# Softplus written back into its PSUM bank, in a kernel of attention, a mixture of experts and a second MLP

## The chip, the core and the metric

The kernel runs on one core of a Trainium2 chip. The metric is the device time of one execution in microseconds, the median of several runs. A page of the profile and a trace come from one more execution, recorded by the hardware profiler.

## The reference

Three stages follow each other. `x` goes from one to the next as 2304 rows of 512 numbers; everything is float32.

```python
# attention over keys and values averaged in groups of 8
attn = softmax(q @ pooled_k.T / 8);  x = attn @ pooled_v      # 4 batches, 8 heads, 576 x 64
# mixture of 8 experts; P comes from 8 rounds of row and column normalisation of exp(x @ w_gate)
for e in range(8):
    h = np.maximum(x @ w1[e], 0.0);  out += P[:, e:e+1] * (h @ w2[e])
# second MLP, with softplus
h = x @ w_in                                                  # 512 -> 2048
g = np.maximum(h, 0.0) + np.log1p(np.exp(-np.abs(h)))
out = g @ w_out                                               # 2048 -> 512
```

The change touches the line with `g`, in the second MLP alone.

## The kernel before

**Engines.** TensorE (PE) multiplies, ScalarE (ACT) applies functions and casts, VectorE (DVE) and GpSimd (POOL) do arithmetic on tiles, SyncE (SP) issues most transfers. PE writes its products to PSUM, which has eight banks of 128 partitions by 512 float32; all other tiles lie in SBUF. GpSimd works on SBUF tiles alone here.

**Precision.** Each float32 operand of a product is split in two: a rounded part (`hi`, type float32r) and a remainder (`lo`). A product is then three matmuls, hi·hi, lo·hi and hi·lo (`three`, L527). So each block of hidden values needs, after its function, a cast (the `hi` part, tile `hhi`) and a subtraction (the `lo` part, tile `hlo`).

**Phases and units.** The tokens are cut in three groups of 768. The work after attention is six phases: the experts for groups 0, 1 and 2 ("moe", 32 units each), then the second MLP for groups 1, 2 and 0 ("sp", 8 units each). A unit takes 256 hidden columns. `first(n)` makes the four hidden blocks of 128 x 384 of unit n with seven products of 6 matmuls (Strassen's scheme; the sums `pa`, `pb`, `pc`, `pd` lie in four banks of kind "p"), so 42 matmuls of 384 columns. `second(n, i)`, for i from 0 to 5, multiplies 128 tokens by the unit's 256 rows of the second weight: 6 matmuls of 512 columns into a bank `py`, which is then added to an accumulator `g` in SBUF (L630 in moe; L615 in sp, but a copy on ScalarE, L613, in the first unit of an sp phase).

**Order.** The kernel writes its order out by hand: `first(n+1)`, then `second(n, 0)` to `second(n, 5)`, then `first(n+2)`, and so on. After `first(n+1)` the activation of its block (0, 0) is issued; the other three are taken from the list `pending`, one behind each of `second(n, 0)`, `second(n, 1)`, `second(n, 2)`. Each engine works its own list in that order. There are three banks of kind "y": `py` of i takes the bank that `py` of i-3 gave back, and gives it back when the addition into `g` has read it. So on VectorE's list a remainder `hlo` stands between two of these additions.

**Weights of the next unit.** ScalarE casts them (`w1hi`, L194; `w2hi`, L202) and GpSimd subtracts (`w1lo`, `w2lo`, helper L165), while `second` runs.

**Side work.** `hook()` takes one entry of a list `side` at each call. In an sp phase it is called 14 times in `first` and 6 times in `second`, in a moe phase 7 and 6 times. At the start of the first two sp phases the list holds the preparation of the next token group: 6 transposes with copies (`pt`, L636, L637), 8 sums (`xs`, L464, L467) and 14 remainders (`xh` on ScalarE, L498; `xl` on VectorE, L503), with empty entries between. That is 92 entries. Their banks `pt`, `xs` and `xh` come from the same three "y" banks as `py`.

**The activation.** `relu` reads its bank twice: ScalarE writes `hhi` from it (L542), and VectorE makes `hlo` from the bank and `hhi` (L543). `softplus` has an extra tile `g` of 128 x 384 float32 in SBUF (tag `sp`, two buffers): ScalarE writes it from the bank (L550), ScalarE casts it to `hhi` (L551), and VectorE subtracts `hhi` from it (L552).

Of the kernel before, what the change touches and what calls it, by code (L numbers as in the profile page):

```python
# [9 lines left out]
F32 = mybir.dt.float32  # L10
F32R = mybir.dt.float32r
U32 = mybir.dt.uint32
AF = mybir.ActivationFunctionType
ALU = mybir.AluOpType
# [5 lines left out]
def attention_moe_softplus_kernel(  # L20
# [12 lines left out]
    nc = tc.nc  # L33
# [512 lines left out]

    def softplus(at, src):
        hh, hl = at
        g = tpool.tile(list(src.shape), F32, tag="sp", name="sp")
        nc.scalar.activation(g, src, AF.Softplus)  # L550
        nc.scalar.copy(hh, g)  # L551
        nc.vector.tensor_tensor(hl, g, hh.bitcast(F32), op=ALU.subtract)  # L552

    def first(n, between):

# [249 lines left out]
    tpool = None  # L805
# [35 lines left out]
    for step, (what, n) in enumerate(todo):  # L841
# [35 lines left out]
        else:  # L877
# [19 lines left out]
            if f + 1 < len(phases) and u == (20 if f == 0 else 8 if kind == "moe" else 0):  # L897
# [5 lines left out]
                else:  # L903
                    g = acc_at[phases.index(("moe", npair))]
# [7 lines left out]
            if attn_m[0] is None and "" in banks:  # L912
                part_banks()
                tpool = pools[0]
# [32 lines left out]
```

## Time and profile before

| | |
|---|---|
| median of 3 runs | 2119.74 us (2118.05 to 2121.77) |
| the profiled execution | 2116.47 us |
| its span, first to last instruction | 2114.7 us |
| TensorE busy | 2024.2 us, 96% |
| VectorE, ScalarE, GpSimd busy | 1442.5, 829.6, 1278.0 us |
| mean granted TensorE clock | 0.985 |

The attention stage fills about the first 105 us (parts of it run on beside the first expert phase), the expert phases last until about 1650 us, and the second MLP fills the rest. Busy times are sums over all of these, so a change in the last stage is read from that stage's rows. In the rows below, a number in square brackets behind an instruction is the time that its engine stood idle before it, and what ended that. [...]

### The profile page before, as it was taken

The page shows a single profiled execution, that of the slowest core. Times are in us where ns is not written, and L with a number is a line of the kernel's source. Part 1 is how long each engine was busy: PE and PEld are TensorE (multiplying, and loading weights), DVE is VectorE, ACT ScalarE, POOL GpSimd, SP SyncE. Part 2 cuts the span into 40 slices and gives each one's busy share as a digit, 9 for nine tenths or more (in the row PEclk, how much of TensorE's full clock was granted, in tenths as well). Part 3 has the DMA queues.
Part 4 walks back from the last instruction along what each step waited for, and adds up shares of the span by engine and source line. Part 5 has one row for each costly group of instructions (what it writes and reads, how often), then busy time and mean ns, then how long its engine had stood idle before and what let it go on. Part 6 is the DMA issues. An engine that isn't in the chain of part 4 may idle for free.

```text
span 2114.7 us, 28374 instructions
## 1 busy us (share of the span) xinstructions
PE 2024.2 (96%) x10643; PEld 1789.4 (85%) x10643; DVE 1442.5 (68%) x2417; ACT 829.6 (39%) x1607; POOL 1278.0 (60%) x1069
## 2 busy tenths in 40 slices
PE   8799999999999999999999999999999988988998
PEld 6687899889889898888898988989889867867877
DVE  3777567776665776677777676667775576576666
ACT  3554434323434224333233333342233554554532
POOL 6654555666665766666666666567576554554653
PEclk8899999999999999999999999999999998999999
DMA  6342221233333333323324333223232323323321
GB/s 175 81 114 70 81 65 60 80 95 110 107 105 109 101 99 113 109 96 99 108 93 152 100 100 92 87 95 109 90 100 85 102 73 105 117 70 126 99 60 60
DMA packets 142311, 205.70 MB, mean 97 GB/s; under 512 B 27916, under 2 KB 88796, under 8 KB 142172
## 3 DMA queue, kind: packets, MB, share of 16 engines
q1 hardware_dynamic: 132092, 190.12, 29.0%
q10 hardware_dynamic: 10080, 13.77, 1.8%
q8 instruction: 83, 1.36, 0.3%
q14 instruction: 56, 0.46, 0.1%
HBM read 173.76 MB, written 30.09 MB: 96 GB/s over the span
## 4 chain that ended last, share of the span: by engine, by line
PE 76%; DVE 10%; POOL 5%; ACT 5%; issue 3%; DMA 1%; ACTq 0%; SPq 0%; POOLq 0%; DVEq 0%
PE py L527 36%; PE p L527 36%; DVE hlo L552 4%; POOL w1lo L165 2%; ACT w1hi L194 2%; DVE g L615 1%; PE s L314 1%; ACT hhi L551 1%; PE px L352 1%; POOL w2lo L165 1%; DVE p L570 1%; POOL sums L165 1%; ACT sp L550 1%; DMA f<-in_moe_w_out_dram 1%; PE pa L342 1%
## 5 line engine op out<-in xcount | busy, mean ns | idle before, releaser
L527 PE MATMUL py<-w2hi,hhi 128*128 128x512 f32 x1440 | 573.6, 398 | 55.1 <-DVE g L615 46.7
L165 POOL TENSOR_TENSOR w1lo<-w1raw,w1hi 128x512 fp32r<-128x512 f32 x240 | 242.5, 1031 | 594.3 <-ACT w1hi L194 594.3
L527 PE MATMUL p<-xhi,w1hi 128*128 128x384 f32 x1680 | 568.4, 338 | 10.6 <-DVE p L570 5.2
L527 PE MATMUL py<-w2hi,hlo 128*128 128x512 f32 x1440 | 569.5, 395 | 0.0
L527 PE MATMUL p<-xlo,w1hi 128*128 128x384 f32 x1680 | 565.4, 337 | 3.8 <-DVE xlo L479 3.8
L527 PE MATMUL py<-w2lo,hhi 128*128 128x512 f32 x1440 | 568.9, 395 | 0.0
L527 PE MATMUL p<-xhi,w1lo 128*128 128x384 f32 x1680 | 565.4, 337 | 3.0 <-POOL w1lo L165 3.0
L630 DVE SCALAR_TENSOR_TENSOR g<-py,prob,g 128x512 f32<-128x512 f32 x468 | 350.0, 748 | 94.0 <-PE py L527 83.0
L527 PEld LDWEIGHTS py<-w2hi,hhi 128*128 128x128 f32 x1440 | 273.1, 190 | 130.9 <-DVE g L615 64.1
L527 PEld LDWEIGHTS p<-xhi,w1hi 128*128 128x128 f32 x1680 | 316.9, 189 | 28.8 <-DVE p L570 7.8
L542 ACT ACTIVATE hhi<-p 128x384 fp32r<-128x384 f32 x384 | 180.8, 494 | 391.0 <-PE p L527 347.4
L527 PEld LDWEIGHTS p<-xlo,w1hi 128*128 128x128 f32 x1680 | 317.0, 189 | 14.4 <-DVE xlo L479 4.5
L527 PEld LDWEIGHTS py<-w2hi,hlo 128*128 128x128 f32 x1440 | 273.0, 190 | 58.8
L527 PEld LDWEIGHTS p<-xhi,w1lo 128*128 128x128 f32 x1680 | 317.1, 189 | 3.6 <-POOL w1lo L165 3.6
L527 PEld LDWEIGHTS py<-w2lo,hhi 128*128 128x128 f32 x1440 | 273.3, 190 | 48.7
L165 POOL TENSOR_TENSOR w2lo<-w2raw,w2hi 128x1024 fp32r<-128x1024 f32 x120 | 294.5, 2455 | 17.1 <-ACT w2hi L202 17.1
L165 POOL TENSOR_TENSOR w1lo<-sums,w1hi 128x1024 fp32r<-128x1024 f32 x120 | 289.0, 2409 | 0.0
L572 ACT COPY za<-p 128x384 f32<-128x384 f32 x120 | 57.8, 482 | 573.7 <-PE p L527 573.7
L543 DVE SCALAR_TENSOR_TENSOR hlo<-p,hhi 128x384 fp32r<-128x384 f32 x384 | 211.0, 550 | 28.9 <-ACT hhi L542 28.8
L570 DVE TENSOR_TENSOR za<-p,za 128x384 f32<-128x384 f32 x120 | 66.9, 557 | 215.1 <-PE p L527 215.1
L552 DVE TENSOR_TENSOR hlo<-sp,hhi 128x384 fp32r<-128x384 f32 x96 | 132.3, 1380 | 39.1 <-ACT hhi L551 39.1
L570 DVE TENSOR_TENSOR u<-p,za 128x384 f32<-128x384 f32 x120 | 66.8, 557 | 123.9 <-PE p L527 94.5
(111 smaller groups left out, 2093.9 us busy)
## 6 DMA issues: line engine op xcount, KB each, us to landing
w1raw<-in_moe_w_dram SPq DMA_DIRECT2D x96, 512.0 KB
w2raw<-in_moe_w_dram SPq DMA_DIRECT2D x96, 512.0 KB
xlod<-xl ACTq DMA_DIRECT2D x70, 192.0 KB
xlo<-xlod SPq DMA_DIRECT2D x35, 384.0 KB
w1raw<-v SPq DMA_DIRECT2D x24, 512.0 KB
w2raw<-v SPq DMA_DIRECT2D x24, 512.0 KB
f<-in_moe_w_in_dram SPq DMA_DIRECT2D x16, 512.0 KB
v<-dt SPq DMA_DIRECT2D x32, 256.0 KB
```

What stands on the lines that cost most here:

```text
L165: nc.gpsimd.tensor_tensor(o, a, b, op=ALU.subtract)
L194: nc.scalar.copy(at(hi), src)
L314: nc.tensor.matmul(ps[:QP, j * 2 * SP:(j + 1) * 2 * SP], qT[:, j * QP:(j + 1) * QP], kb)
L342: nc.tensor.transpose(pa[:SP, j * QP:(j + 1) * QP], ex[:, 2 * j + h, :], ident[:QP, :QP])
L352: nc.tensor.matmul(px[h * D:(h + 1) * D, :W], vp[:, h, :], aT[:, h, :])
L527: nc.tensor.matmul(ps, lhs[a], rhs[b], start=first and i == 0, stop=last and i == 2, skip_group_check=goes_on,)
L542: nc.scalar.activation(hh, src, AF.Relu)
L543: nc.vector.scalar_tensor_tensor(hl, src, 0.0, hh.bitcast(F32), op0=ALU.max, op1=ALU.subtract)
L552: nc.vector.tensor_tensor(hl, g, hh.bitcast(F32), op=ALU.subtract)
L570: add = lambda o, x, y: nc.vector.tensor_tensor(o, x, y, op=ALU.add)
L572: nc.scalar.copy(a, pa)
L630: nc.vector.scalar_tensor_tensor(a, py, prob[:, t, e:e + 1], a, op0=ALU.mult, op1=ALU.add)
```

## The change

The tile `g` goes. ScalarE writes the softplus back into the bank that it read, casts from there, and VectorE subtracts with the bank as its first operand.

```diff
     def softplus(at, src):
         hh, hl = at
-        g = tpool.tile(list(src.shape), F32, tag="sp", name="sp")
-        nc.scalar.activation(g, src, AF.Softplus)
-        nc.scalar.copy(hh, g)
-        nc.vector.tensor_tensor(hl, g, hh.bitcast(F32), op=ALU.subtract)
+        nc.scalar.activation(src, src, AF.Softplus)
+        nc.scalar.copy(hh, src)
+        nc.vector.tensor_tensor(hl, src, hh.bitcast(F32), op=ALU.subtract)
```

No instruction is added, taken away or moved on any engine: 96 softplus, 96 casts and 96 subtractions stand where they stood, with other operands. ScalarE's list in the middle of the last sp phase, from a unit's second block on to the next unit's first (`p_...` are the four banks of a unit), before:

```order
L550 ACTIVATE sp<-p_19048 128x384
L551 CAST hhi<-sp 128x384
L550 ACTIVATE sp<-p_19050 128x384
L551 CAST hhi<-sp 128x384
L202 CAST w2hi<-w2raw 128x1024
L550 ACTIVATE sp<-p_19049 128x384
L551 CAST hhi<-sp 128x384
L572 COPY za<-p_19188 128x384
```

and after:

```order
L549 ACTIVATE p_18964<-p_18964 128x384
L550 CAST hhi<-p_18964 128x384
L549 ACTIVATE p_18966<-p_18966 128x384
L550 CAST hhi<-p_18966 128x384
L202 CAST w2hi<-w2raw 128x1024
L549 ACTIVATE p_18965<-p_18965 128x384
L550 CAST hhi<-p_18965 128x384
L571 COPY za<-p_19100 128x384
```

Only the operands differ (the line numbers fall by one, and the banks' numbers count fewer tiles). A bank of kind "p" is now read last by VectorE's subtraction, where ScalarE's softplus read it last, so it is that which TensorE must wait for before it writes the bank again. The waits of TensorE's matmuls into the second and third bank of a unit in the same phase, before:

```order
L527 MATMUL p_18012<-xhi,w1hi 128x384 [waits Activation_49]
L527 MATMUL p_18012<-xlo,w1hi 128x384
L527 MATMUL p_18012<-xhi,w1lo 128x384 [waits Pool_49]
L527 MATMUL p_18013<-xhi,w1hi 128x384 [waits Activation_49]
L527 MATMUL p_18013<-xlo,w1hi 128x384
```

and after:

```order
L527 MATMUL p_17956<-xhi,w1hi 128x384 [waits Activation_49]
L527 MATMUL p_17956<-xlo,w1hi 128x384
L527 MATMUL p_17956<-xhi,w1lo 128x384 [waits Pool_49]
L527 MATMUL p_17957<-xhi,w1hi 128x384
L527 MATMUL p_17957<-xlo,w1hi 128x384
```

(rows between the two banks' first matmuls repeat and are left out). The matmul into the third bank has lost its wait for ScalarE and got none for VectorE, since a matmul ahead of it in the list waits for a later VectorE instruction already. The wait that stays at the second bank is for the weights' cast.

## Rows read from the trace of the kernel before

**Rows 1.** The page: busy tenths of TensorE in 40 slices of the span.
```profile
PE   8799999999999999999999999999999988988998
```
**Rows 2.** Windows, one of sp, one of moe: length, busy of each engine, clock.
```profile
1656.50:2110.40 453.90, 403.34 (x1920) 347.08 (x1918) 295.03 (x389) 211.76 (x396) 238.75 (x181) 0.97 0.27 86
...
1000.00:1640.00 640.00, 637.45 (x3202) 574.63 (x3202) 454.41 (x778) 221.01 (x409) 418.64 (x347) 1.00 0.32 102
```
**Rows 3.** Waits of PE, 1650 to the end: total us, times, longest.
```profile
PE py L527 <- DVE g L615: 46.7, 35, 3.7
```
**Rows 4.** Timeline of a plain sp unit: start, length, instruction, [idle before].
```profile
2043.54 2.40 POOL L165 TENSOR_TENSOR w1lo<-sums,w1hi 128x1024 fp32r<-128x1024 f32 x1
...
2043.72 2.63 DVE L552 TENSOR_TENSOR hlo<-sp,hhi 128x384 fp32r<-128x384 f32 x1 [0.78 <-ACT hhi L551]
2044.11 0.51 ACT L551 CAST hhi<-sp 128x384 fp32r<-128x384 f32 x1
2044.53 1.05 ACT L202 CAST w2hi<-w2raw 128x1024 fp32r<-128x1024 f32 x1
2045.90 2.69 POOL L165 TENSOR_TENSOR w2lo<-w2raw,w2hi 128x1024 fp32r<-128x1024 f32 x1
2046.28 0.68 DVE L615 TENSOR_TENSOR g<-py,g 128x512 f32<-128x512 f32 x1
...
2046.88 2.13 DVE L552 TENSOR_TENSOR hlo<-sp,hhi 128x384 fp32r<-128x384 f32 x1
...
2047.01 0.50 PE L527 MATMUL py<-w2hi,hhi 128*128 128x512 f32 x1 [0.55 <-DVE g L615]
...
2049.67 0.50 PE L527 MATMUL py<-w2hi,hhi 128*128 128x512 f32 x1 [0.99 <-DVE g L615]
```
**Rows 5.** Tiles: count, min/median/max ns, first and last start, forms.
```profile
L527 PE MATMUL py<-w2hi,hlo x1440: 387/389/632, 111.9 to 2110.0; 128*128 128x512 f32 x180
L543 DVE SCALAR_TENSOR_TENSOR hlo<-p,hhi x384: 512/549/560, 100.6 to 1647.2; 128x384 fp32r<-128x384 f32 x192
L552 DVE TENSOR_TENSOR hlo<-sp,hhi x96: 541/832/2634, 1657.6 to 2099.5; 128x384 fp32r<-128x384 f32 x96
...
L503 DVE TENSOR_TENSOR xl<-g,xh x70: 536/545/555, 532.5 to 1934.3; 128x384 fp32r<-128x384 f32 x70
...
L550 ACT ACTIVATE sp<-p x96: 476/488/493, 1656.5 to 2097.9; 128x384 f32<-128x384 f32 x96
L551 ACT CAST hhi<-sp x96: 511/513/515, 1657.0 to 2098.5; 128x384 fp32r<-128x384 f32 x96
...
L542 ACT ACTIVATE hhi<-p x384: 470/492/532, 96.4 to 1646.1; 128x384 fp32r<-128x384 f32 x192
...
L464 ACT COPY xs<-g x40: 474/487/508, 500.7 to 1869.3; 128x384 f32<-128x384 f32 x40
```
**Rows 6.** Timeline of ACT: the copy `za`, once in each unit.
```profile
1385.77 0.48 ACT L572 COPY za<-p 128x384 f32<-128x384 f32 x1 [2.29 <-PE p L527]
1401.90 0.48 ACT L572 COPY za<-p 128x384 f32<-128x384 f32 x1 [3.44 <-PE p L527]
...
1635.76 0.48 ACT L572 COPY za<-p 128x384 f32<-128x384 f32 x1 [5.93 <-PE p L527]
1651.30 0.48 ACT L572 COPY za<-p 128x384 f32<-128x384 f32 x1 [4.70 <-PE p L527]
...
2087.81 0.48 ACT L572 COPY za<-p 128x384 f32<-128x384 f32 x1 [5.01 <-PE p L527]
```
**Rows 7.** Chain of waits: four transposes in moe, and the last matmuls.
```profile
1304.35 0.44 PE pt L636 x4
...
2095.40 15.02 PE py L527 x66
```
**Rows 8.** Timeline of an sp unit with side work.
```profile
1737.61 2.57 DVE L552 TENSOR_TENSOR hlo<-sp,hhi 128x384 fp32r<-128x384 f32 x1 [1.08 <-ACT hhi L551]
...
1740.83 0.79 PE L527 MATMUL py<-w2hi,hhi 128*128 128x512 f32 x1 [3.69 <-DVE g L615]
```

## The prediction, made before the changed kernel ran

> **What bounds the kernel now.** I read the page's slices first [rows 1]: TensorE is busy for nine tenths or more in every slice from the third to the 32nd, and falls to eight in most of those after that. The sp phases lie there, and `softplus` runs nowhere else. Then a window of each kind [rows 2]: of 640 us of moe TensorE is idle for 640 - 637.45 = 2.6 us, at a clock of 1.00; of 453.9 us of sp for 453.9 - 403.34 = 50.6 us, at 0.97. So TensorE bounds moe, and something else bounds sp.
>
> TensorE's waits name it [rows 3]: 46.7 of the 50.6 us are 35 waits for L615, the addition that gives a `py` bank back. What makes L615 late is read from one unit [rows 4]. Its subtraction `hlo` starts at 2043.72, while GpSimd works on a `w1lo` from 2043.54 to 2045.94, and ends at 2046.35, 0.4 us after it. The next starts at 2046.88 under a `w2lo` that ends at 2048.59, and ends at 2049.01, again 0.4 us after it. The additions queue behind both, and TensorE waits 0.55 and 0.99 us for them. By tile, L552 takes 0.54 us at least, 0.83 in the median and 2.63 at most, while L543 and L503, which read one operand from a bank, stay within 0.51 and 0.56 us in 384 and 70 instructions [rows 5], though GpSimd is at work for 418.61 of 640 us there [rows 2]. So the subtraction with two operands in SBUF is what GpSimd holds up; one with an operand in PSUM is not.
>
> **How much time there is to win.** `za` starts once in each unit. In moe the period is 1651.30 - 1635.76 = 15.54 us [rows 6]. From 1651.30 to 2087.81 there are 23 sp periods: 436.51 us. At TensorE's pace they would take 23 x 15.54 = 357.4 us, and the 48 transposes of the side work 12 x 0.44 = 5.3 us [rows 7], together 362.7. The excess is 73.8 us. It splits in 50.6 us of waits, 453.9 x 0.03 = 13.6 us of lower clock [rows 2], and a rest of 9.6 us: 0.25 us behind each of some 39 waits, where the first matmul takes 0.50 us [rows 4] rather than the usual 0.39 [rows 5]. The lower clock belongs to the long waits: after 3.69 us without work the first matmul takes 0.79 us [rows 8]. Behind 2087.81 there is nothing to win: the last 66 matmuls run without a gap in 15.02 us, 0.228 each [rows 7].
>
> **The change, part by part.**
>
> *The subtraction.* 96 times it gets one operand from a bank. Nearest rows: L503, the same operation with one operand in each memory, 0.536 to 0.555 us, and L543, 0.512 to 0.560. I take 0.55. Bounds: 0.51, and 0.83 with 2.63 at most, as now, if the hold-up has another cause (rival B). In a plain unit [rows 4]: subtraction from 2043.72 to 2044.27, addition (0.68) to 2044.95; the next cast ended at 2044.62, so subtraction to 2045.50 and addition to 2046.18. TensorE wanted the first bank at 2047.01 - 0.55 = 2046.46 and will want the second 6 x 0.228 = 1.37 us later, at 2047.83. Both are free 1.5 us early, so a plain unit waits for nothing and runs at 15.54 us.
>
> [...]
>
> *The softplus and the cast.* ScalarE in place in a bank is not in the trace. It reads a bank and writes SBUF in 0.488 us (L550) and reads SBUF and writes a bank in 0.487 (L464). If reading and writing go on together, 0.47 to 0.51 us; if they take turns, the sum, 0.98. I take 0.49, since each of the two rows already reads and writes at once. The cast from a bank should take 0.47 to 0.53 (L542) rather than 0.513 (L551): nothing. What hides ScalarE now is its idle time (211.76 us busy of 453.9 [rows 2]). At 0.98 the second block's subtraction comes 0.5 and the third's 1.0 us later, within the 1.5 us that the plain unit has left; in units with side work it would add about 0.7 us each.
>
> *The tile `g`.* With it goes ScalarE's wait for one of its two buffers. The bank is held longer instead, until the subtraction. The fourth block is the last: its subtraction would end at about 2047.2 in the unit of [rows 4] (its softplus follows the weight cast that ends at 2045.58, and softplus, cast and subtraction are 1.55 us), and TensorE's next product into that bank starts 12 matmuls after the next unit's first, which follows six matmuls from 2047.83, so not before 2049.2. The 12 take (15.54 - 36 x 0.228) / 42 = 0.175 us each, which makes it 2051.3. Four microseconds are left, and TensorE's list holds no new wait there.
>
> *GpSimd* gets its time back too (a `w2lo` takes 2.69 us here), but nothing waits for it in sp. *Transfers* must bring a unit's weights each 15.54 us instead of each 436.51 / 23 = 19.0: moe does the same at that pace.
>
> **What stays.** In the two batches of side work `xh`, `xs` or `pt` takes one of the three "y" banks between two `py`, so that TensorE waits for an addition one step earlier. 92 entries at 20 a unit are 4.6 units a batch, 9.2 in all (these counts are from the code). Three prices. From moe, where the side work makes a period 16.13 us (1401.90 - 1385.77 [rows 6]): 0.6 x 9.2 = 5.4 us. From the sp unit of [rows 8]: the subtraction there shrinks by 2.57 - 0.55 = 2.0 us, which leaves 3.69 - 2.0 = 1.7 of the wait, so 1.7 x 9.2 = 15.6. Between them: moe's 0.6 at 20 calls a unit instead of 13, 0.6 x 20 / 13 = 0.9, and some 0.2 for the cast that stands in ScalarE's chain beside the softplus, so 1.1 x 9.2 = 10 us. I take 10. Waits of that size cost no clock: after 0.99 us the first matmul takes 0.50 us [rows 4], after 3.69 us 0.79 [rows 8].
>
> **Sum.** 2116.47 (profiled execution; 1.8 us of it outside the span) - 73.8 + 10 = 2052.7 us. The median shown is 2119.74, 3.3 us above that execution, and the changed kernel is timed like the median: 2056, rounded to 2055. From the two ends for the side work, 2119.74 - 73.8 + 5.4 = 2051 to 2061; with nothing left over 2046, with ScalarE at 0.98 us in place 2061 + 6 = 2067. The forecast's own range is 2046 to 2067.
>
> **Rivals.**
>
> *A, the stall moves into the side work.* The longer ScalarE chain (softplus, then cast) and the shared "y" banks become the wait in the 9.2 units: 3 us each, and some lower clock again, about 30 to 35 us stay. For it: these units wait longest now (3.69 us against 0.99). Against: moe, with the same banks, loses 0.6 us a unit. 2119.74 - 73.8 + 33 = 2079, or 2067 to 2080.
>
> *B, the subtraction stays held up* because it is the read of `hhi` or the write of `hlo` in SBUF that GpSimd delays, not the pair of operands. Then nothing goes: 2116 to 2121. Against it stand 454 instructions of L543 and L503 that read and write SBUF in the same way and never take over 0.56 us.
>
> *C, slower: the banks come back too late.* TensorE waits at the head of a unit until VectorE has subtracted the last block. It costs time only if that subtraction is over 4 us later than worked out above, and to lose the 73.8 us again a further 73.8 / 23 = 3.2 us a unit. So from 7.2 us of delay on the kernel is slower; at 8 us it is about 2119.74 + 23 x 0.8 = 2138. For it: VectorE's list is in order, and all else waits on it. Against: without the hold-up VectorE has far less to do than TensorE (295.03 of 453.9 us even with it [rows 2]). [...]
>
> **How the numbers follow.** The forecast gets 0.84, A 0.10, B 0.03, C 0.03. A measurement of this kernel tells about 0.2% (4.2 us) from no change. Forecast and A are faster: 0.94; B is the same: 0.03; C slower: 0.03. The range reaches from 2044, a little below the time with nothing left over, to 2074, which takes in the forecast's upper end and half of A.
>
> **What the profile of the changed kernel would show.** Right: L551 (now the subtraction) 96 times within 0.51 and 0.57 us; TensorE's waits for L614 (now the addition) down from 46.7 to about 10 us, all in the units with side work; `za` periods of 15.54 us in plain units; a clock near 1.00 in sp. ScalarE's softplus at about 0.49 us shows the in-place price right, 0.98 wrong. The prediction is wrong if the subtraction still takes over 1 us under GpSimd's work (B), if 3 us waits stay in the side work (A), or if matmuls into the "p" banks wait for VectorE's subtraction (C).

## The result, and the profile after

| | before | changed |
|---|---|---|
| median | 2120.55 us (4 runs, 2118.05 to 2121.77) | 2062.34 us (4 runs, 2060.18 to 2067.60) |
| ratio | | 0.9731, 95% interval 0.9709 to 0.9752 |
| profiled execution, its span | 2116.47, 2114.7 us | 2063.60, 2061.8 us |

The kernel is 58 us faster. That is about 7 us short of the 2055 us that were forecast, and within the range of 2044 to 2074. (The median of before has one run more than in the table ahead of the prediction.)

TensorE's row of the page's 40 slices has lost its dip in the sp phases [rows 1]:

```profile
PE   8898999999999999999999999999999999999999
```

The next row is a window up to the last matmul (length, busy of each engine with its count, then clock, DMA share, GB/s). It starts 6.2 us ahead of the first softplus, where the window of before starts with it; TensorE works through these 6.2 us without a gap. So the two can be compared in what TensorE does not do: 401.00 - 389.85 = 11.2 us without work, where it was 50.6, at a clock of 1.00 for 0.97 [rows 2] (the granted share of TensorE's clock, a mean over the window). VectorE is busy for 219.61 us in place of 295.03:

```profile
1656.50:2057.50 401.00, 389.85 (x1956) 347.85 (x1954) 219.61 (x392) 207.09 (x398) 220.95 (x184) 1.00 0.31 99
```

What TensorE waited for in that stretch, in all, times, longest [rows 3]:

```profile
PE py L527 <- DVE g L614: 8.9, 8, 1.6
PE py L527 <- DVE g L467: 2.3, 2, 1.1
```

The tile view of the activation (count, then min/median/max ns) answers to [rows 5]. The subtraction has a spread of 17 ns, where it had one of 2.1 us:

```profile
L549 ACT ACTIVATE p<-p x96: 458/482/502, 1662.7 to 2043.8; 128x384 f32<-128x384 f32 x96
L550 ACT CAST hhi<-p x96: 478/480/483, 1663.2 to 2044.3; 128x384 fp32r<-128x384 f32 x96
L551 DVE TENSOR_TENSOR hlo<-p,hhi x96: 543/556/560, 1663.7 to 2046.0; 128x384 fp32r<-128x384 f32 x96
```

The timeline of a plain unit answers to [rows 4]. GpSimd is at work on the same tiles at the same place, and all three subtractions under it take 0.55 to 0.56 us; no matmul into `py` waits in this unit:

```profile
2012.60 2.42 POOL L165 TENSOR_TENSOR w1lo<-sums,w1hi 128x1024 fp32r<-128x1024 f32 x1
...
2012.76 0.56 DVE L551 TENSOR_TENSOR hlo<-p,hhi 128x384 fp32r<-128x384 f32 x1 [0.69 <-ACT hhi L550]
...
2013.24 0.68 DVE L614 TENSOR_TENSOR g<-py,g 128x512 f32<-128x512 f32 x1
...
2013.84 0.55 DVE L551 TENSOR_TENSOR hlo<-p,hhi 128x384 fp32r<-128x384 f32 x1
...
2014.98 2.40 POOL L165 TENSOR_TENSOR w2lo<-w2raw,w2hi 128x1024 fp32r<-128x1024 f32 x1
...
2015.50 0.56 DVE L551 TENSOR_TENSOR hlo<-p,hhi 128x384 fp32r<-128x384 f32 x1 [0.52 <-ACT hhi L550]
```

The copy `za`, once a unit, answers to [rows 6]. The first row is the first sp unit, the next three lie in the first batch of side work, the last two at the end:

```profile
1657.48 0.48 ACT L571 COPY za<-p 128x384 f32<-128x384 f32 x1 [4.70 <-PE p L527]
...
1725.73 0.48 ACT L571 COPY za<-p 128x384 f32<-128x384 f32 x1 [4.98 <-PE p L527]
1743.18 0.48 ACT L571 COPY za<-p 128x384 f32<-128x384 f32 x1 [3.64 <-PE p L527]
1760.63 0.48 ACT L571 COPY za<-p 128x384 f32<-128x384 f32 x1 [3.64 <-PE p L527]
...
2019.41 0.48 ACT L571 COPY za<-p 128x384 f32<-128x384 f32 x1 [3.95 <-PE p L527]
2034.95 0.48 ACT L571 COPY za<-p 128x384 f32<-128x384 f32 x1 [3.95 <-PE p L527]
```

From the first to the last of the 24 it is 377.47 us, for 436.51 before: 59.0 us less. Against the 362.7 us of TensorE's own pace an excess of 14.8 us is left of 73.8. Plain units have the period 15.54. Of each batch of side work, the unit with the transposes has 20.2 (some 2.65 us of it are the transposes themselves, half of the prediction's 5.3), the next 16.95, and two with remainders to make have 17.45. In one of these two TensorE waits once, where it waited 3.69 us [rows 8]:

```profile
1737.67 0.50 PE L527 MATMUL py<-w2hi,hhi 128*128 128x512 f32 x1 [1.57 <-DVE g L614]
```

The two profiled executions differ by 52.9 us and not by 59.0, since the first sp unit starts 6.2 us later in the new one (1657.48 for 1651.30).

### The profile page after: what moved, and what is told of

It reads as the page before. It is cut to its first block, busy times and chain, and to the rows that moved or that the text cites. A ratio compares the mean times of both kernels' runs of the same rounds, so it can differ in the third digit from the quotient of the medians.

```text
span 2061.8 us, 28361 instructions
## 1 busy us (share of the span) xinstructions
PE 2010.8 (98%) x10643; PEld 1788.7 (87%) x10643; DVE 1364.5 (66%) x2417; ACT 822.5 (40%) x1607; POOL 1258.2 (61%) x1069
## 4 chain that ended last, share of the span: by engine, by line
PE 83%; DVE 5%; POOL 5%; ACT 3%; issue 3%; DMA 1%; SPq 0%; ACTq 0%; DVEq 0%; POOLq 0%
PE py L527 41%; PE p L527 37%; POOL w1lo L165 2%; PE s L314 1%; ACT w1hi L194 1%; PE px L352 1%; POOL w2lo L165 1%; PE pk L297 1%; POOL sums L165 1%; PE pa L342 1%; DMA f<-in_moe_w_out_dram 1%; DVE p L569 1%; DVE za L569 0%; PE pq L283 0%; DMA f<-in_moe_w_in_dram 0%
## 5 line engine op out<-in xcount | busy, mean ns | idle before, releaser
L527 PE MATMUL py<-w2hi,hhi 128*128 128x512 f32 x1440 | 565.9, 393 | 15.7 <-DVE g L614 8.9
L165 POOL TENSOR_TENSOR w1lo<-w1raw,w1hi 128x512 fp32r<-128x512 f32 x240 | 241.8, 1029 | 556.1 <-ACT w1hi L194 556.1
L165 POOL TENSOR_TENSOR w2lo<-w2raw,w2hi 128x1024 fp32r<-128x1024 f32 x120 | 289.5, 2412 | 14.8 <-ACT w2hi L202 14.8
L165 POOL TENSOR_TENSOR w1lo<-sums,w1hi 128x1024 fp32r<-128x1024 f32 x120 | 289.4, 2411 | 0.0
L202 ACT CAST w2hi<-w2raw 128x1024 fp32r<-128x1024 f32 x120 | 126.5, 1054 | 0.0
```

The lines of the kernel that those rows point to most:

```text
L165: nc.gpsimd.tensor_tensor(o, a, b, op=ALU.subtract)
L202: nc.scalar.copy(hi, raw)
L527: nc.tensor.matmul(ps, lhs[a], rhs[b], start=first and i == 0, stop=last and i == 2, skip_group_check=goes_on,)
```

## The experiments

Two questions were open: is it GpSimd's reading that held up a subtraction with two operands in SBUF, and what makes the 14.8 us that stay? All medians are of several runs, with the kernel before run beside them on the same chip (2120.8 to 2121.9 us). "Excess" is the time from the first to the last `za` of the sp phases over 362.7 us, in the profiled execution.

| run | median us | ratio to before, 95% interval | excess us | first `za` at |
|---|---|---|---|---|
| before | 2120.55 | 1 | 73.8 | 1651.30 |
| changed | 2062.34 | 0.9709 to 0.9752 | 14.8 | 1657.48 |
| e0_again | 2060.35 | 0.9704 to 0.9733 | 14.8 | 1654.31 |
| e1_four_buffers | 2119.45 | 0.9984 to 1.0004 | 73.2 | 1656.29 |
| e2_write_only | 2064.22 | 0.9721 to 0.9750 | 17.4 | 1655.43 |
| e8_fill_beside | 2065.31 | 0.9716 to 0.9754 | 16.3 | 1658.17 |
| e3_copy_to_bank | 2081.31 | 0.9800 to 0.9830 | 33.0 | 1657.02 |
| e7_no_softplus | 2052.79 | 0.9660 to 0.9686 | 6.6 | 1656.43 |
| e4_side_bank | 2052.00 | 0.9655 to 0.9682 | 6.2 | 1657.16 |
| e5_late_w1 | 2062.88 | 0.9709 to 0.9735 | 15.1 | 1656.47 |
| e6_both | 2051.11 | 0.9651 to 0.9677 | 3.1 | 1656.73 |

**e0_again: the changed kernel once more.**

> The changed kernel once more, word for word. It asks where the part of the time lies that the sp phases don't explain: in the first trace of the changed kernel its first sp unit starts 6.2 us later than in that of before (za at 1657.48 against 1651.30), though nothing ahead of it was changed. Theory: the opening attention stage differs from execution to execution, so the start of the first sp unit moves by some us again, while the stretch from the first to the last za stays at 377.5 us within 1 us. Rival: the change itself costs those 6 us, and the first sp unit starts at 1657 to 1658 again, and at 1651 in every kernel that keeps the tile g. Time 2060 to 2068.

The first and the last `za` of its sp phases:

```profile
1654.31 0.48 ACT L571 COPY za<-p 128x384 f32<-128x384 f32 x1 [4.70 <-PE p L527]
...
2031.78 0.48 ACT L571 COPY za<-p 128x384 f32<-128x384 f32 x1 [3.95 <-PE p L527]
```

The stretch is 377.47 us again, to the hundredth, while its start moved by 3.2 us. The table's last column has 1654.3 to 1658.2 in all new executions, in the three that subtract from `g` in SBUF as before too (e1, e2, e8). So the opening varies whatever `softplus` does, and the profiled execution of before was an early one. The difference is there before the expert phases are under way: their first subtraction `hlo` starts at 100.6 us in the execution of before, at 107.0 in that of the changed kernel and at 104.3 in this one.

**e1_four_buffers: before, with four buffers for `g`.**

```diff
-        g = tpool.tile(list(src.shape), F32, tag="sp", name="sp")
+        g = tpool.tile(list(src.shape), F32, tag="sp", name="sp", bufs=4)
```

> The kernel before, with four buffers for the tile g in place of two, so that ScalarE's softplus never waits for VectorE's subtraction; the subtraction still has both operands in SBUF. Theory (GpSimd holds up a subtraction with two operands in SBUF): the subtraction still takes up to 2.6 us, TensorE still waits about 45 us for the additions, 2112 to 2121 us. Rival (the change won by taking away the wait for one of two buffers): 2060 to 2080 us.

Its subtraction, from the tile view, and TensorE's waits in sp:

```profile
L552 DVE TENSOR_TENSOR hlo<-sp,hhi x96: 540/832/2634, 1662.6 to 2103.9; 128x384 fp32r<-128x384 f32 x96
```
```profile
PE py L527 <- DVE g L615: 45.9, 34, 3.7
```

Both are those of before, and so is the time. The tile's two buffers were no part of the stall.

**e2_write_only: before, with GpSimd filling `w1lo` and `w2lo` with zeros in the sp phases.**

```diff
-            pool_sub(at(lo), src, at(hi).bitcast(F32))
+            if sets[n][1] == "sp":
+                nc.gpsimd.memset(at(lo).bitcast(F32), 0.0)
+            else:
+                pool_sub(at(lo), src, at(hi).bitcast(F32))
```

(and likewise for `w2lo`)

> The kernel before, in which GpSimd fills w1lo and w2lo of the sp phases with zeros where it made them by a subtraction; so the remainders of those weights are left out of the result. GpSimd still writes the same tiles in SBUF but reads nothing for them. Theory (it is GpSimd's reading that holds up VectorE's second operand in SBUF): the subtraction hlo stays near 0.54 us except under the four short sums of a unit, which still read, and the time falls to 2055 to 2070 us. Rival (any work of GpSimd in SBUF, writes too, holds it up): the subtraction is stretched by the length of a fill, and with fills of about 1 us the time is 2080 to 2115 us.

The time is what the theory said, but the run doesn't tell the two apart. A fill waits for no cast, so it ran at another time than the subtractions, as the timeline of a unit shows (its last subtraction, then the fills):

```profile
2016.26 0.56 DVE L558 TENSOR_TENSOR hlo<-sp,hhi 128x384 fp32r<-128x384 f32 x1 [0.59 <-ACT hhi L557]
...
2018.18 1.67 POOL L196 MEMSET w1lo<- 128x512 f32 x3
2019.79 0.96 POOL L207 MEMSET w2lo<- 128x1024 f32 x1
```

What it shows is that with GpSimd's long subtractions gone the old `softplus`, with `g` in SBUF, is nearly as fast as the new one: 2 us more in the median, 2.6 in the excess. The tile view has a spread left:

```profile
L558 DVE TENSOR_TENSOR hlo<-sp,hhi x96: 541/558/1125, 1661.7 to 2046.6; 128x384 fp32r<-128x384 f32 x96
```

The subtractions over 0.56 us, up to 1.12, are all among the 22 that started under one of GpSimd's short sums (L162, L165), which still read; the 66 with no work of GpSimd beside them take 0.55 to 0.56.

**e8_fill_beside: the fills again, now at the subtractions' place.**

```diff
+    def fill(lo, src, hi):
+        first = (slice(None),) * (len(lo.shape) - 1) + (slice(0, 1),)
+        pool_sub(lo[first], src[first], hi[first].bitcast(F32))
+        for _ in range(2):
+            nc.gpsimd.memset(lo.bitcast(F32), 0.0)
```

(called in the sp phases in place of the subtractions of `w1lo` and `w2lo`)

> The kernel before once more with zeros in place of the weights' remainders in the sp phases, since in the run with fills alone GpSimd made them at another time than VectorE's subtractions. Here each fill stands behind a subtraction of 2 to 8 elements a partition, which waits for the cast as the whole subtraction did, and is done twice, so that it is at work where the whole subtraction was (about 1.2 us for a w1lo of 512, 1.9 for one of 1024). Nearly all of the weights' remainders are left out of the result. Theory (GpSimd's reading holds up VectorE's second operand in SBUF): the fills lie over the subtractions hlo and these still take 0.54 to 0.6 us in the median and at most 1.1 (under the short sums, which read): 2058 to 2068 us. Rival (GpSimd's writing does it too): subtractions under a fill end after it, some at 1.2 to 2.2 us, TensorE waits 15 to 40 us for the additions: 2075 to 2110 us.

Timeline of a unit, then its subtraction in the tile view:

```profile
2015.72 1.97 POOL L174 MEMSET w1lo<- 128x1024 f32 x2
2016.10 0.55 DVE L564 TENSOR_TENSOR hlo<-sp,hhi 128x384 fp32r<-128x384 f32 x1
2017.66 0.19 POOL L165 TENSOR_TENSOR w2lo<-w2raw,w2hi 128x2 fp32r<-128x2 f32 x1
2017.85 0.56 DVE L564 TENSOR_TENSOR hlo<-sp,hhi 128x384 fp32r<-128x384 f32 x1 [0.60 <-ACT hhi L563]
2017.91 1.96 POOL L174 MEMSET w2lo<- 128x1024 f32 x2
```
```profile
L564 DVE TENSOR_TENSOR hlo<-sp,hhi x96: 547/558/564, 1664.4 to 2048.1; 128x384 fp32r<-128x384 f32 x96
```

The fills lie over the third and the fourth subtraction, which have both operands in SBUF and take 0.55 us all the same. Of the 96, 54 started while a fill was at work, and none takes over 0.564. So GpSimd's writing does not hold them up. Its subtractions and sums, which read as well, do: up to 2.63 us under them in the kernel before, up to 1.12 in e2.

**e3_copy_to_bank: before, with a copy of `g` into the bank for the subtraction.**

```diff
         nc.scalar.copy(hh, g)
-        nc.vector.tensor_tensor(hl, g, hh.bitcast(F32), op=ALU.subtract)
+        nc.scalar.copy(src, g)
+        nc.vector.tensor_tensor(hl, src, hh.bitcast(F32), op=ALU.subtract)
```

> The kernel before, with its tile g, its softplus and its cast as they were; ScalarE then also copies g into the bank, and VectorE subtracts from the bank. So the place of VectorE's operand is changed alone, at the price of a copy of about 0.49 us behind each cast. Theory (the operand's place is what counts): the subtraction takes 0.54 to 0.56 us 96 times; plain units have 1.5 us to spare and ScalarE's chain is 0.5 us longer at the second block and 1.0 at the third, so they stay at 15.54 us, and the units with side work lose 0.5 to 1 us more than in the changed kernel: 2062 to 2072 us. Rival (ScalarE writing in place, or the tile that went, made the gain): 2100 us or more.

```profile
L553 DVE TENSOR_TENSOR hlo<-p,hhi x96: 546/558/560, 1663.7 to 2064.4; 128x384 fp32r<-128x384 f32 x96
```

The subtraction is as theory has it, by its operand's place alone, under the same work of GpSimd. The plain units are at 15.54 us but for one in each phase, at 16.3, where TensorE waits 0.5 us for a `py` that ScalarE copies (L614). The time is a miss: the copy costs 9 us more than the upper end that was expected. In a unit with remainders to make TensorE waits 2.47 us, where it waits 1.57 in the changed kernel, and then once more, where the changed kernel has no wait:

```profile
1741.15 0.50 PE L527 MATMUL py<-w2hi,hhi 128*128 128x512 f32 x1 [2.47 <-DVE g L616]
...
1744.80 0.50 PE L527 MATMUL py<-w2hi,hhi 128*128 128x512 f32 x1 [0.60 <-DVE g L616]
```

The first wait is 0.90 us longer for two copies of 0.48 us: ahead of the addition that gives this bank back stand the copies of the unit's first and second block. With the second wait and the restart behind it (0.25 by the prediction's estimate) that makes nearly all of the 1.77 us by which the unit's period is longer (19.22 for 17.45).

**e7_no_softplus: the changed kernel without the softplus instruction.**

> The changed kernel without the softplus instruction: the second MLP's hidden values go on as they are, so the function is left out of the result. ScalarE's chain is 0.48 us shorter for each block, while banks, casts and subtractions stay. It asks how much the units with side work feel the chain's length, in which the copy to a bank (0.48 us more for each block) cost 19 us over the changed kernel. If the chain's length sets the waits in these units: periods of 16.5 to 17 us there, 2053 to 2058 us. If the shared banks alone do: 2060 to 2063 us.

`za` in the first batch of side work:

```profile
1739.19 0.48 ACT L570 COPY za<-p 128x384 f32<-128x384 f32 x1 [4.63 <-PE p L527]
1755.59 0.48 ACT L570 COPY za<-p 128x384 f32<-128x384 f32 x1 [4.63 <-PE p L527]
```

The period is 16.40 us there for 17.45, so 1.05 us less for 0.48 us a block, twice over again. An excess of 0.86 us a unit is left with a chain as long as that of `relu`. The unit with the transposes gains more: its period (from the first to the second `za` below) is 20.22 us in the changed kernel,

```profile
1688.56 0.48 ACT L571 COPY za<-p 128x384 f32<-128x384 f32 x1 [0.47 <-PE p L527]
1708.78 0.48 ACT L571 COPY za<-p 128x384 f32<-128x384 f32 x1 [2.89 <-PE p L527]
```

and 18.33 here, 1.89 us less:

```profile
1687.50 0.48 ACT L570 COPY za<-p 128x384 f32<-128x384 f32 x1 [0.47 <-PE p L527]
1705.83 0.48 ACT L570 COPY za<-p 128x384 f32<-128x384 f32 x1 [3.01 <-PE p L527]
```

The unit behind it gains nothing (16.96 for 16.95). Over both batches the excess falls by 8.2 us, from 14.8 to 6.6.

**e4_side_bank: the changed kernel, with `xs` and `xh` in the bank of kind "c".**

```diff
-                    got.append(bank("xh", dt=F32R)[:, :src.shape[2]])
+                    got.append(bank("xh", side_kind(), F32R)[:, :src.shape[2]])
```

(`side_kind()` gives "c" in the sp phases and "y" elsewhere; `xs` likewise)

> The changed kernel, with the side work's sums and remainders (xs, xh) of the sp phases in the bank of kind c, which nothing else uses there, so that they take none of the three y banks from py. Theory (what stays of the stall, 14.8 us over 23 periods in the changed kernel, comes from the shared y banks): periods of 15.5 to 15.9 us in the units with side work, TensorE's waits for the additions near 0 in place of 8.9 us, 2047 to 2054 us. Rival (it comes from the long chain on ScalarE and VectorE in these units, whatever the banks): the same periods of 17.4 us, 2060 to 2064 us; and with one bank in place of three the side work may get slower.

```profile
PE py L532 <- DVE g L619: 3.7, 6, 1.4
```

The excess falls by 8.6 us, from 14.8 to 6.2, and the median to 2052.0. The units with remainders have 16.1 us and not 15.5 to 15.9; the two ahead of them have 18.3 and 17.3. So the shared banks are part of it and not all. This run and e7 take 8.6 and 8.2 us away, which is more than 14.8 together. That fits a wait that needs both, a bank that is wanted a step early and a long chain ahead of the addition that gives it back, so that taking either away shortens it.

**e5_late_w1: the changed kernel, with the casts `w1hi` behind the second block's softplus and cast.**

```diff
+            if kind == "sp" and n + 1 < len(sets):
+                late.append(n + 1)
+            else:
+                prep_w1(n + 1)
+                load_w(1, n + 2)
...
                 if pending:
                     pending.pop(0)()
+                if late:
+                    prep_w1(late[0])
+                    load_w(1, late.pop() + 1)
```

> The changed kernel, with the three casts w1hi (and the subtractions and the load behind them) issued in the sp phases behind the second block's softplus and cast rather than ahead of them. ScalarE's list before the second addition gets 1.9 us shorter. Theory (in the units with side work TensorE waits for the second addition, which stands behind the second subtraction, which waits for ScalarE): the 17.4 us periods fall to 16.2 to 16.8 us and TensorE's waits from 8.9 to 4 us, 2052 to 2058 us. Rival (the shared y banks alone): 2060 to 2064 us. Plain units stay at 15.54 us by both, unless GpSimd's w1lo then comes too late for the next unit.

A miss: the time stays. The wait did fall where it was expected to, from 1.57 to 0.44 us, but ScalarE's 1.9 us of casts now stand ahead of the third block, and two more waits come up in the same unit:

```profile
1735.52 0.50 PE L527 MATMUL py<-w2hi,hhi 128*128 128x512 f32 x1 [0.44 <-DVE g L614]
1737.55 0.50 PE L527 MATMUL py<-w2hi,hhi 128*128 128x512 f32 x1 [0.36 <-DVE g L614]
1739.40 0.49 PE L527 MATMUL py<-w2hi,hhi 128*128 128x512 f32 x1 [0.19 <-DVE g L614]
```

They are 0.99 us in all. Of the period's excess, 17.42 - 15.54 = 1.88 us, the restarts behind them would be most of the rest: three at the 0.25 us of the prediction make 0.75.

**e6_both: the edits of e4 and e5.**

> The edits of the two runs before it together: side work in the bank of kind c, and the casts w1hi behind the second block. If either theory holds, nearly all of the 14.8 us goes: 2046 to 2052 us. It can't get lower than about 2045 by these two, since TensorE's own pace (15.54 us a unit) then sets all sp periods.

```profile
PE py L532 <- DVE g L619: 0.5, 2, 0.3
```

The lowest median of all: 2051.11 us, 0.9664 of before (0.9651 to 0.9677), and an excess of 3.1 us. Its interval lies below that of the changed kernel, but it overlaps that of e4, so what the late casts add to the bank is seen in the excess (6.2 to 3.1 us) and not in the medians.

## Why the prediction was right, and where it was off

- **What bounded sp.** Right. The 46.7 us of waits for the addition came from the subtraction under GpSimd, and went with it (8.9 us left). Shown by e3 (the operand's place alone frees the subtraction: 0.560 us at most), e1 (the buffers are no cause: 2.63 at most, 45.9 us of waits), e2 (without GpSimd's long subtractions the old form is fast: 0.558 in the median, 10.3 us of waits) and e8 (with GpSimd writing over it, too: 0.564 at most, 9.8 us of waits).
- **The subtraction, 0.55 us.** Right: 0.556 in the median, and 0.558 from SBUF where GpSimd does not hold it up (e8), so that the bank as its source cost nothing. (GpSimd's 418.61 us of 640 in the prediction are 418.64 in [rows 2].)
- **ScalarE in place.** Right, at the low end: 0.482 us for the softplus and 0.480 for the cast, which was 0.513 from SBUF. Taking turns at 0.98 did not happen.
- **Plain units at 15.54 us.** Right. The additions of the unit shown ended at 2013.92 and 2014.98, and no matmul waited.
- **The clock.** Right: 1.00 in place of 0.97. The longest wait in sp is 1.6 us, where it was 3.7; in e3, with waits of up to 2.5 us, the same window has 1.00 too.
- **The bank's longer hold (rival C).** No matmul into a "p" bank waits in the sp phases: the 8.9 and 2.3 us of waits shown above, all at `py`, are all that TensorE has there.
- **What stays, 10 us.** This term was mis-sized: 14.8 us, just inside the upper end of 15.6 that [rows 8] gave. The wait there came out at 1.57 us for the 1.7 worked out. The 10 us were two parts, and e7 tells them apart. The part scaled from moe, 0.9 x 9.2 = 8.3 us, was somewhat high: without the softplus 6.6 us stay. What failed is the step "some 0.2 for the cast that stands in ScalarE's chain", 0.2 x 9.2 = 1.8 us: the longer chain costs 8.2 us, 1.05 us in each unit with remainders and 1.89 in the one with the transposes. In the units with remainders the chains of two blocks stand ahead of the addition that is waited for, so that 0.48 us a block count twice.
- **The sum.** From the profiled execution's own time: 2116.47 - 73.8 + 14.8 = 2057.5, and 2063.6 was measured. The other 6.2 us are the opening, which was early in the execution from which all terms were taken. The 3.3 us between that execution and the median were taken along without knowing their place, and were too few. So the 2055.9 us that the prediction had ahead of rounding fell short of this execution by 7.7 us: 4.8 of what stays, and 2.9 of the opening.

## What to carry to other kernels

Look at the spread of one instruction in the tile view before its mean: here a minimum of 0.54 and a maximum of 2.63 us for the same shape suggested that something shared held it up, and the instruction of another engine that ended 0.4 us before it ended was the first suspect. Where a VectorE subtraction with two SBUF operands ran beside GpSimd's subtractions, an operand left in its PSUM bank took it out of the way (0.83 us in the median before, 0.556 after), at the price of holding the bank longer, which no matmul waited for here. A term for "what stays" is better taken from the unit where the wait stands, with each instruction of the chain counted as often as it stands ahead of that wait, than scaled from another stage.

## What the runs showed of the hardware beyond the prediction

- In the sp phases of before, a VectorE subtraction with two SBUF operands that started under a GpSimd subtraction or sum ended behind it: 66 of the 96 start under one and none of them ends before it; the 48 of these that take 1.1 us or more, up to 2.63, all end 0.41 to 0.42 us after it. Five that started 0.22 to 0.35 us ahead of a GpSimd subtraction took 0.55 us.
- A fill on GpSimd over such a subtraction cost it nothing (0.547 to 0.564 us in e8).
- ScalarE's cast was faster from a bank, 0.480 us (0.486 in e7, where ScalarE had not written it), than from SBUF, 0.513, and softplus in place (0.482) was no slower than into SBUF (0.488).
- The stretch of the sp phases took the same time in two executions of the changed kernel (377.47 us, though single periods differ by up to 0.06), while its start moved by 3.2 us between them, and over the executions of all ten new runs from 1654.3 to 1658.2.
